# Attention into experts: the last chunk's values ahead of the tenth chunk's gate, three weight splits moved

## The chip, the cores and the metric

The kernel runs on one core of a Trainium2 chip. The time is the device time of one execution in microseconds (us), and the figure of a kernel is the median of its runs. For the kernel before, the three runs shown are 331.6, 331.83 and 452.45 us, so the median is 331.83 us. Its profiled execution is one more run, which took 332.76 us.

## The reference

Three layers follow each other, all in float32.

1. Attention with a decaying state, for 2 x 8 heads, 768 steps and head size 48: `y[t] = r[t] @ (state + (u*k[t]) v[t]^T)`, then `state = w * state + k[t] v[t]^T`.
2. A layer of 8 experts over the 1536 x 384 result: `logits = x @ w_gate`; each token goes to the expert with the largest logit (`argmax`), takes the next free place of that expert in the order of the tokens, and is dropped once the expert's capacity (384) is full; an expert computes `relu(x @ w1[e]) @ w2[e]` with 1024 hidden columns; the result is weighted by the token's softmax probability.
3. A dense layer: `h = x @ w_in`, `h * softmax(h)`, a normalization over the 1024 columns, times `g_ln`, `@ w_out`.

## The kernel before, in words

**Chunks.** Attention works on 12 chunks (`m` = 0 to 11, `NM` = 12) of 128 tokens, six of each batch entry. Below, "chunk 10" is `m` = 10, which the change's title calls the tenth. For each chunk, `values(m)` (L317) and `attend(m)` (carry L330, attended L340) write the output of attention, transposed, into two PSUM tiles; two ScalarE copies `ys` (L346) evict them; `tokens(m)` (L395) turns them back into tokens with the gate's logits beside them (`xp`). `state(m)` (L378, L381) makes the state of the next chunk, and `decay(m)` (L366) scales it ahead.

**The gate.** `gate1(m)` reduces the logits on VectorE (L404 to L414) to a one-hot row of the chosen expert (`oh_all`), then takes the exponentials on ScalarE (`ex`, L417, sum `gs`). `ranks(m)` (L427 to L430) counts, by three small matmuls, the place of each token within its expert. `gate2(m)` takes the reciprocal `gate` (L446), picks the rank (`junk`, L449), makes the slot (L452, L455) and scales the tokens (`whole`, `xg`, L464, ScalarE). `scatter(m)` (L485) writes the slot's table by an indirect DMA on GpSimd, and `store(m)` (L480) the tokens by a DMA on SyncE's queue.

**The first expert's tokens.** The first expert does not wait for its tokens to travel through DRAM. For chunks 0 to 7 they are gathered early (`xe0`, L94, in chunk 9) and transposed into the PSUM tile `x0` (L662). For chunks 8 to 11 they are placed by matmuls: `place(i)` makes a 0/1 matrix `P` (L559, VectorE), `part(i)` and `other(i)` make a high and a low part of the tokens (`xh`, L565 or L568 on ScalarE; `xl`, L574 on GpSimd for chunks 8 to 10, L578 on VectorE for chunk 11), and `add` (L655) adds three matmuls of 224 columns for each chunk and part into `x0`. Then `xhi`, `xlo` (L688, L690) split `x0` for the experts' matmuls.

**Experts.** Each of the 8 experts has four groups `g` of its hidden columns. `mm1(g)` (L813) makes 18 matmuls of 224 columns into `hps`, evicted as `hh` (L819, ScalarE) and `hl` (L820, VectorE). `mm2(g)` (L799 to L801) uses them two groups later. Weights are float32 and come in halves (`raw`, five buffers, L107, SyncE's queue); `split_q(kind, g, ...)` makes of one quarter a high part `whi` (L116, ScalarE) and a low part `wlo` (L122, VectorE). With `defer=True` it issues only the high part and hands back the low part as a function, kept in `pend`. The second expert's tokens are gathered through the slot table (`load_ids`, L86, then `xe`, L94) and transposed by TensorE (`xt`, L792) ahead of `mm2(2)`. A second set of weights (`load_piece`, L140) is decoded on VectorE and ScalarE between the experts' groups.

**Order.** The order of each engine's instructions is that of the program (`manual_schedule`): nothing is rearranged, each engine takes its instructions in turn and waits on semaphores. `together` takes its generators' steps in rotation.

In the kernel before, `split_q(1, 0)` and `split_q(1, 1)` are issued at the end of chunks 4 and 5, their low parts in the middle of chunks 5 and 6; `split_q(2, 0)` is issued in chunk 10 with its low part behind `gate1(10)`. Chunk 11 is the loop's last turn: its `attend` comes behind `gate1(10)`, and `ranks(10)` stands between `attend(11)` and `tokens(11)`.

Of the kernel before, what the change touches and what calls it, by code (L numbers as in the profile page):

```python
# [21 lines left out]
NM = N // C  # L22
# [6 lines left out]
LAST = 4  # L29
# [6 lines left out]
def rwkv_moe_solu_kernel(  # L36
# [75 lines left out]
    def split_q(kind, g, by_dma, defer=False):  # L112
        raw = raw_t[kind, g // 2][:, (g % 2) * 768:(g % 2 + 1) * 768]
        hi = wsp.tile([128, 768], F32R, tag=f"hi{kind}", name=f"whi{kind}_{g}", bufs=2 + kind)
        lo = wsp.tile([128, 768], F32R, tag=f"lo{kind}", name=f"wlo{kind}_{g}", bufs=2 + kind)
        S.activation(hi, raw, AF.Copy)  # L116
        def low():
            if by_dma:
                s = (w1 if kind == 1 else w2)[g // 4, :, g // 2 % 2, (g % 2) * 768:(g % 2 + 1) * 768]
                G.dma_start(out=lo, in_=s, accum_op=ALU.add)  # L120
            else:
                V.tensor_tensor(lo, raw, hi.bitcast(F32), ALU.subtract)  # L122

        if by_dma:
            S.activation(lo, raw, AF.Copy, scale=-1.0)  # L125
        if not defer:
            low()
        n = 3 if kind == 1 else 2
        (w1s if kind == 1 else w2s)[g] = tuple(t.rearrange("p (a f) -> p a f", a=n) for t in (hi, lo))
        return low  # L130
# [5 lines left out]
    def load_piece(p, eng=nc.sync):  # L136
        t = w64_p.tile([128, 384, 2], I32, tag="w64", name=f"w64_{p}")
        s = (w_in if p < NP else w_out).rearrange("p a f -> p (a f)").bitcast(I32)
        j = p % NP
        eng.dma_start(out=t.rearrange("p n c -> p (n c)"), in_=s[:, j * 768:(j + 1) * 768])  # L140
        pieces[p] = t

    def attention(actx):
# [281 lines left out]
        def ranks(m):  # L425
            rp = banks.pop(m)[2]
            T.matmul(rp, mask_b, oh_all[:, m, :], start=True, stop=False)  # L427
            if m:
                T.matmul(rp, ones_b, oh_all[:, m - 1, :], start=False, stop=False)
            T.matmul(rp, ones_b, accs[max(m - 1, 0)], start=False, stop=True)  # L430
            rps[m] = rp
# [3 lines left out]
        def gate2(m):  # L435
            gs = gst.pop(m)
            oh, rk1 = oh_all[:, m, :], rank_all[:, m:m + 1]
            t1 = firsts[m]
            last = m == NM - 1
            if m + 2 < NM:  # L440
                acc = sm.tile([128, NE], BF16, tag="acc", name=f"acc{m}")
                G.tensor_tensor(acc, accs[m], oh, ALU.add)
                accs[m + 1] = acc
            yield
            gate = sm.tile([128, 1], F32, tag="gate", name=f"gate{m}")
            V.reciprocal(gate, gs)  # L446
            raw[m] = xps.pop(m)[:, :, 0:2 * D], gate
            junk = sm.tile([128, NE], F32, tag="junk", name=f"junk{m}")
            V.scalar_tensor_tensor(junk, rps.pop(m), 1.0, oh, ALU.mult, ALU.mult, accum_out=rk1)  # L449
            yield  # L450
            t2 = sm.tile([128, 1], F32, tag="t2", name=f"t2{m}")
            V.tensor_scalar(t2, rk1, float(cap), float(2 * NX), ALU.is_ge, ALU.mult)  # L452
            yield
            slot = sm.tile([128, 1], I32, tag="slot", name=f"slot{m}")
            V.tensor_scalar(slot, rk1, t1, t2, ALU.add, ALU.add)  # L455
            slots[m] = slot
            yield
            if not last:
                whole(m)
            yield  # L460

        def whole(m):
            xg = a2.tile([128, HP, 2 * D], F32, tag="xg", name=f"xg{m}", bufs=LAST + 1)
            S.activation(xg, raw[m][0], AF.Copy, scale=raw[m][1])  # L464
            xgs[m] = xg.rearrange("p a d -> p (a d)")

        def together(*steps):
            steps = list(steps)
            while steps:
                for s in list(steps):  # L470
                    if next(s, steps) is steps:
                        steps.remove(s)
# [82 lines left out]
        onehots, his, los = {}, {}, {}  # L555

        def place(i):
            P0 = sm.tile([128, W], F32R, tag="P0", name=f"P0_{i}", bufs=LAST)
            V.tensor_scalar(P0, iota_w, firsts[i], rank_all[:, i:i + 1], ALU.subtract, ALU.is_equal)  # L559
            return P0  # L560

        def part(i):
            xh = sm.tile([128, DM], F32R, tag="xh", name=f"xh{i}", bufs=LAST)
            if i < NM - 2:
                S.activation(xh, xgs[i], AF.Copy)  # L565
            else:
                xp, gate = raw[i]
                S.activation(xh.rearrange("p (a d) -> p a d", a=HP), xp, AF.Copy, scale=gate)  # L568
            return xh

        def other(i, xh):
            xl = sm.tile([128, DM], F32R, tag="xl", name=f"xl{i}", bufs=LAST)
            if i < NM - 1:
                G.tensor_tensor(xl, xgs[i], xh.bitcast(F32), ALU.subtract)  # L574
            else:
                xp, gate = raw[i]
                three = lambda t: t.rearrange("p (a d) -> p a d", a=HP)
                V.scalar_tensor_tensor(three(xl), xp, gate, three(xh).bitcast(F32), ALU.mult, ALU.subtract)  # L578
            return xl

        halves = {2: (1, 0), 4: (2, 0), 5: (1, 1), 6: (2, 1), 7: (1, 2), 8: (2, 2)}
        first = {4: (1, 0), 5: (1, 1)}
        pend = []
        for m in range(NM):
            values(m)
            if m:
                if m + 1 < NM:
                    scores(m + 1)
                if m + 2 < NM:
                    prelude(m + 2)  # L590
                if m + 1 < NM:
                    mask_scores(m + 1)
            attend(m, lambda: ranks(m - 1) if m else None)
            if m == NM - 2:
                state(m)
            if m == NM - 1:
                onehots[m - 2] = place(m - 2)
                steps = gate2(m - 1)
                for _ in range(4):
                    next(steps)  # L600
                his[m - 1] = part(m - 1)
                together(steps)
            elif m:
                together(gate2(m - 1))
            if m == NM - LAST + 1:
                xe0 = load_xe(0, 0, 2, 1 + (NM - LAST) * C, ld.tile([128, 3, DM], F32, tag="krv", name="xe0"))
            if m:
                scatter(m - 1)
            if m == NM - 1:
                los[m - 1] = other(m - 1, his[m - 1])  # L610
            if m < NM - 2:
                state(m)
            while pend:
                pend.pop()()
            if m == NM - 2:
                pend.append(split_q(2, 0, False, defer=True))
            if m + 2 < NM:
                products = prelude2(m + 2)
                next(products)
            if m < NM - 2:  # L620
                decay(m + 1)
            tokens(m)
            if m + 2 < NM:
                together(gate1(m), products)
                weigh(m + 2)
                prelude3(m + 2)
            elif m + 1 < NM:
                together(gate1(m))
                pend.pop()()
            if NM - LAST < m < NM - 1:  # L630
                if m < NM - 2:
                    onehots[m - 1] = place(m - 1)
                his[m - 1] = part(m - 1)
                los[m - 1] = other(m - 1, his[m - 1])
            chunks.pop(m)
            if m + 4 < NM:
                load_chunk(m + 4)
            if m:
                store(m - 1)
            if m in halves:  # L640
                load_half(*halves[m])
            if m == NM - LAST:
                load_ids(0, 1)
            if m >= NM - 2:
                load_piece(m - NM + 2)
            if m in first:
                pend.append(split_q(*first[m], False, defer=True))


        m = NM - 1  # L650
        x0 = ps_s.tile([128, KD, 256], F32, tag="s", name="x0")[:, :, 0:W]

        def add(i, t):
# [12 lines left out]
        for i in (m - 3, m - 2):  # L666
            add(i, his)
            add(i, los)
        together(gate1(m))
        ranks(m)  # L670
        onehots[m - 1] = place(m - 1)
        steps = gate2(m)
        next(steps), next(steps), next(steps)
        his[m] = part(m)
# [25 lines left out]
    def experts_and_solu():  # L700
# [208 lines left out]
        dec = None  # L909
        most = []  # L910
        split_q(1, 2, False)
        split_q(2, 1, False)
        load_half(1, 3)
        for g in range(NQ + 2):
# [8 lines left out]
            tokens = q == (2 if e else 3) and e + 1 < NE  # L923
# [291 lines left out]
```

## Time and profile before

| | |
|---|---|
| median of the runs shown | 331.83 us |
| the profiled execution | 332.76 us |
| its span, first to last instruction | 331.0 us |
| granted TensorE clock, mean | 0.987 of full |
| TensorE busy | 314.9 us, 95% |
| VectorE busy | 241.8 us, 73% |
| ScalarE busy | 186.5 us, 56% |
| GpSimd busy | 149.7 us, 45% |

The busy shares are means over the whole span. Attention takes its first 77 us, the experts follow until about 216 us, the dense layer is the rest. Times in the rows below are counted from the first instruction. PE is TensorE's matmuls, PEld its weight loads, DVE is VectorE, ACT ScalarE, POOL GpSimd, SP SyncE. A bracket such as `[0.97 <-ACT ex L417]` is the idle time of the engine ahead of the row and what ended it.

### The profile page before, as it was taken

The numbers are of one execution on the slowest core, as the hardware profiler recorded it, in microseconds if no ns is written. First come the engines' busy times: TensorE is split into PE (matmuls) and PEld (weight loads), VectorE is DVE, ScalarE is ACT, GpSimd is POOL, SyncE is SP. The second block draws the span as 40 slices with busy tenths as digits, with TensorE's granted clock in tenths as the row PEclk, the third lists the DMA queues.
The fourth block names the chain that finished last, engine by engine and source line by source line (L and its number), as shares of the span: only waits on it lengthen the run. The fifth ranks groups of instructions, "written<-read, shape, count | busy, mean of one in ns | idle before, by whom it ended". The sixth has DMA issues, their size and how long they took to land. (4 is left out here: it accounts for less than half of the span.)

```text
span 331.0 us, 7339 instructions
## 1 busy us (share of the span) xinstructions
PE 314.9 (95%) x2736; PEld 290.5 (88%) x2736; DVE 241.8 (73%) x555; ACT 186.5 (56%) x406; POOL 149.7 (45%) x198
## 2 busy tenths in 40 slices
PE   8899989969999999999999999999999999999990
PEld 3688778859999999999999999978999999999990
DVE  7899999866999999898999896258745555434310
ACT  2545555556659796868686867126455434444420
POOL 7989899571443232323233364414254222333321
PEclk9999999998999999999999999999999999999996
DMA  6999999342877998988898923100000000000010
GB/s 207 398 331 296 345 386 396 130 142 78 267 282 240 313 297 283 286 290 274 283 282 290 271 70 47 14 2 1 0 26 25 26 24 24 26 24 24 26 48 24
DMA packets 20395, 56.24 MB, mean 170 GB/s; under 512 B 6594, under 2 KB 9028, under 8 KB 20356
## 3 DMA queue, kind: packets, MB, share of 16 engines
q1 hardware_dynamic: 16916, 47.67, 40.9%
q0 software_dynamic: 3440, 8.06, 10.1%
q8 instruction: 23, 0.38, 0.5%
q14 instruction: 16, 0.13, 0.1%
HBM read 50.56 MB, written 5.16 MB: 168 GB/s over the span
## 5 line engine op out<-in xcount | busy, mean ns | idle before, releaser
L122 DVE TENSOR_TENSOR wlo<-raw,whi 128x768 fp32r<-128x768 f32 x57 | 52.4, 954 | 1.5 <-ACT whi L116 1.1
L801 PE MATMUL yps<-hh,wlo 128*128 128x224 f32 x192 | 52.8, 275 | 0.1
L799 PE MATMUL yps<-hh,whi 128*128 128x224 f32 x192 | 52.7, 274 | 0.0
L800 PE MATMUL yps<-hl,whi 128*128 128x224 f32 x192 | 52.6, 274 | 0.0
L116 ACT ACTIVATE whi<-raw 128x768 fp32r<-128x768 f32 x64 | 50.6, 838 | 0.0
L1040 POOL TENSOR_SCALAR e<-e,nmu 128x1024 f32<-128x1024 f32 x12 | 13.5, 1124 | 62.7 <-DVE nmu L1039 59.6
L1017 DVE TENSOR_REDUCE nm<-h 128x1 f32<-128x1024 f32 (+1 forms) x13 | 14.7, 1140 | 33.0 <-PE h L1006 30.0
L801 PEld LDWEIGHTS yps<-hh,wlo 128*128 128x128 f32 x192 | 36.9, 192 | 0.3 <-DMA wlo<-in_w 0.3
L800 PEld LDWEIGHTS yps<-hl,whi 128*128 128x128 f32 x192 | 36.9, 192 | 0.0
L799 PEld LDWEIGHTS yps<-hh,whi 128*128 128x128 f32 x192 | 36.9, 192 | 0.0
L120 POOL DMA_DIRECT2D wlo<-in_w x7 | 6.9, 985 | 64.9 <-ACT wlo L125 64.9
L1074 PE MATMUL o<-w_hi,shi 128*128 128x384 f32 x96 | 33.1, 345 | 0.0
L1075 PE MATMUL o<-w_lo,shi 128*128 128x384 f32 x96 | 32.2, 335 | 0.0
L1076 PE MATMUL o<-w_hi,slo 128*128 128x384 f32 x96 | 32.2, 335 | 0.0
L94 POOL DMA_INDIRECT xe<-xs,ids x16 | 21.0, 1311 | 19.2 <-PE xt L792 8.0
L813 PE MATMUL hps<-xhi,whi 128*128 128x224 f32 x192 | 27.5, 278 | 0.4 <-ACT xhi L688 0.4
L813 PE MATMUL hps<-xlo,whi 128*128 128x224 f32 x192 | 26.7, 275 | 0.0
L813 PE MATMUL hps<-xhi,wlo 128*128 128x224 f32 x192 | 26.6, 274 | 0.0
L819 ACT ACTIVATE hh<-hps 128x448 fp32r<-128x448 f32 x32 | 17.3, 539 | 16.4 <-PE hps L813 15.2
L813 PEld LDWEIGHTS hps<-xhi,whi 128*128 128x128 f32 x192 | 24.1, 192 | 0.6 <-ACT xhi L688 0.5
L813 PEld LDWEIGHTS hps<-xhi,wlo 128*128 128x128 f32 x192 | 24.0, 192 | 0.0
L813 PEld LDWEIGHTS hps<-xlo,whi 128*128 128x128 f32 x192 | 24.0, 192 | 0.0
(183 smaller groups left out, 783.8 us busy)
## 6 DMA issues: line engine op xcount, KB each, us to landing
raw<-in_w SPq DMA_DIRECT2D x32, 768.0 KB
krv<-in_krv SPq DMA_DIRECT2D x11, 576.0 KB
rkT<-in_rkT SPq DMA_DIRECT2D x12, 512.0 KB
w<-in_w_in SPq DMA_DIRECT2D x8, 384.0 KB
w<-in_w_out SPq DMA_DIRECT2D x8, 384.0 KB
wlo<-in_w POOLq DMA_DIRECT2D x7, 384.0 KB
xs<-xg SPq DMA_DIRECT2D x12, 192.0 KB
krv<-in_krv SPq DMA_DIRECT2D x1, 384.0 KB
```

Source lines behind the costliest of these rows:

```text
L94: nc.gpsimd.indirect_dma_start(out=t[0:n, b, :], out_offset=None, in_=xs[0:rows, :], in_offset=bass.IndirectOffsetOnAxis(ap=ids[0:n, e, c: ...
L116: S.activation(hi, raw, AF.Copy)
L122: V.tensor_tensor(lo, raw, hi.bitcast(F32), ALU.subtract)
L799: T.matmul(ps, w[0][ws], x[0][xsl], start=first, stop=False, skip_group_check=True)
L800: T.matmul(ps, w[0][ws], x[1][xsl], start=False, stop=False, skip_group_check=True)
L801: T.matmul(ps, w[1][ws], x[0][xsl], start=False, stop=last, skip_group_check=True)
L813: T.matmul(ps[:, f], w1s[g][i][:, kk, wf], x[j][:, kk], start=not (i or j or f or kk), stop=j == 1 and kk == KD - 1, skip_group_check=True,)
L819: S.activation(hh, ps, AF.Relu)
L1017: V.tensor_reduce(nms[j], ps, AX.X, ALU.max, negate=True)
L1074: T.matmul(ps, hi[:, f % 4], wo[0][:, f], start=f == 0, stop=False)
L1075: T.matmul(ps, hi[:, f % 4], wo[1][:, f], start=False, stop=False)
L1076: T.matmul(ps, lo[:, f % 4], wo[0][:, f], start=False, stop=f == KF - 1)
```

## The change

The loop over chunks ends with `m` = 10. Within chunk 10, `values(11)` and `attend(11)` now stand ahead of `gate1(10)`, without `ranks(10)` in them. Behind the loop come `tokens(11)`, then `ranks(10)`, `place(9)`, the first two steps of `gate2(10)` (the second is the reciprocal, which has a step of its own now) and `part(10)`. Then, as before, the transposes of `xe0`, `add` for chunks 8 and 9, and `gate1(11)`; only behind these the rest of `gate2(10)` with `scatter(10)`, `other(10)`, `store(10)`, `load_piece(1)`, `place(10)` and `ranks(11)`. Since the reciprocal is a step, three steps of `gate2(11)` now reach to the rank; the two small instructions of the slot come behind `other(11)` and `whole(11)`.

Of the weight splits, `split_q(1, 0)` and `split_q(1, 1)` are issued in chunks 5 and 6 behind `state(m)`, with their low parts behind `gate1(m)` of the same chunk; `split_q(2, 0)` is issued at the begin of the experts, between `split_q(1, 2)` and `split_q(2, 1)`.

```diff
             raw[m] = xps.pop(m)[:, :, 0:2 * D], gate
+            yield
             junk = sm.tile([128, NE], F32, tag="junk", name=f"junk{m}")
...
-        first = {4: (1, 0), 5: (1, 1)}
+        first = {5: (1, 0), 6: (1, 1)}
         pend = []
-        for m in range(NM):
+        for m in range(NM - 1):
...
-            if m == NM - 1:
-                onehots[m - 2] = place(m - 2)
-                steps = gate2(m - 1)
-                for _ in range(4):
-                    next(steps)
-                his[m - 1] = part(m - 1)
-                together(steps)
-            elif m:
+            if m:
                 together(gate2(m - 1))
...
-            if m == NM - 1:
-                los[m - 1] = other(m - 1, his[m - 1])
             if m < NM - 2:
                 state(m)
-            while pend:
-                pend.pop()()
-            if m == NM - 2:
-                pend.append(split_q(2, 0, False, defer=True))
+            if m in first:
+                pend.append(split_q(*first[m], False, defer=True))
...
-            elif m + 1 < NM:
+            else:
+                values(m + 1)
+                attend(m + 1, lambda: None)
                 together(gate1(m))
+            while pend:
                 pend.pop()()
-            if NM - LAST < m < NM - 1:
+            if NM - LAST < m:
...
         m = NM - 1
+        tokens(m)
+        ranks(m - 1)
+        onehots[m - 2] = place(m - 2)
+        steps = gate2(m - 1)
+        next(steps), next(steps)
+        his[m - 1] = part(m - 1)
...
         together(gate1(m))
+        together(steps)
+        scatter(m - 1)
+        los[m - 1] = other(m - 1, his[m - 1])
+        store(m - 1)
+        load_piece(1)
+        onehots[m - 1] = place(m - 1)
         ranks(m)
-        onehots[m - 1] = place(m - 1)
...
         split_q(1, 2, False)
+        split_q(2, 0, False)
         split_q(2, 1, False)
```

## Rows read from the trace of the kernel before

**Rows 1.** Windows: busy us of each engine (instructions), PEclk, DMA share, GB/s.
```profile
25.00:50.00 25.00, 23.44 (x363) 19.91 (x362) 23.97 (x77) 13.42 (x50) 23.53 (x24) 1.00 0.97 343
...
69.50:72.90 3.40, 2.02 (x19) 1.92 (x19) 2.38 (x11) 2.55 (x9) 2.62 (x3) 1.00 0.43 124
72.90:76.40 3.50, 3.50 (x21) 3.43 (x20) 2.23 (x10) 1.23 (x5) 1.14 (x2) 0.51 0.60 171
...
78.00:85.00 7.00, 7.00 (x61) 6.87 (x62) 6.21 (x13) 6.20 (x13) 1.36 (x3) 1.00 0.51 143
```

**Rows 2.** Timeline of PE, 68 to 78 us: start, us, engine, line, operation, tiles.
```profile
68.04 1.08 PE L340 MATMUL yp<-A,krv 128*48 128x128 f32 x16
70.09 0.17 PE L427 MATMUL xp<-oh_all,mask_b 128*128 128x8 bf16 x1 [0.97 <-ACT ex L417]
...
71.10 1.14 PE L395 MATMUL xp<-sel,ys 112*128 112x104 f32 x8 [0.79 <-ACT ys L346]
...
73.72 0.84 PE L655 MATMUL x<-P,xh 128*128 128x224 f32 x3
74.36 0.84 PE L655 MATMUL x<-P,xl 128*128 128x224 f32 x3
...
76.47 0.49 PE L655 MATMUL x<-P,xh 128*128 128x224 f32 x3
76.83 0.59 PE L655 MATMUL x<-P,xl 128*128 128x224 f32 x3
...
77.87 1.20 PE L813 MATMUL hps<-xhi,whi 128*128 128x224 f32 x6 [0.37 <-ACT xhi L688]
```

**Rows 3.** Timeline of ACT, chunks 10 and 11.
```profile
69.68 0.27 ACT L417 ACTIVATE ex<-xp,nmx 128x8 f32<-128x8 f32 x1 [0.80 <-DVE oh_all L414]
...
70.69 0.64 ACT L346 ACTIVATE ys<-yp 112x256 f32<-112x256 f32 x2
...
75.54 0.58 ACT L568 ACTIVATE xh<-xp,gate 128x384 fp32r<-128x384 f32 x1 [1.35 <-DVE junk L449]
```

**Rows 4.** Timeline of DVE, chunks 10 and 11.
```profile
67.04 0.36 DVE L381 TENSOR_TENSOR Sc<-st,Sw 128x192 f32<-128x192 f32 x1 [1.82 <-PE xp L395]
...
69.51 0.95 DVE L122 TENSOR_TENSOR wlo<-raw,whi 128x768 fp32r<-128x768 f32 x1
...
71.19 0.27 DVE L455 TENSOR_SCALAR slot<-rank_all,t,t 128x1 int32<-128x1 f32 x1
72.28 0.20 DVE L404 TENSOR_REDUCE xp<-xp 128x8 f32<-128x32 f32 x1 [0.82 <-PE xp L395]
...
73.19 0.23 DVE L414 TENSOR_SCALAR oh_all<-xp,m 128x8 bf16<-128x8 f32 x1
...
75.33 0.17 DVE L449 SCALAR_TENSOR_TENSOR junk<-xp,oh_all 128x8 f32<-128x8 f32 x1 [1.03 <-PE xp L430]
...
76.16 0.62 DVE L578 SCALAR_TENSOR_TENSOR xl<-xp,gate,xh 128x384 fp32r<-128x384 f32 x1
76.69 0.27 DVE L455 TENSOR_SCALAR slot<-rank_all,t,t 128x1 int32<-128x1 f32 x1
```

**Rows 5.** Timeline of POOL, chunks 10 and 11.
```profile
72.03 0.99 POOL L485 DMA_INDIRECT idx<-row,slot  x1 [0.16 <-issue]
73.04 1.02 POOL L574 TENSOR_TENSOR xl<-xg,xh 128x384 fp32r<-128x384 f32 x1
77.23 0.99 POOL L485 DMA_INDIRECT idx<-row,slot  x1 [3.18 <-DVE slot L455]
```

**Rows 6.** Timeline of ACT, chunk 6.
```profile
48.91 0.27 ACT L417 ACTIVATE ex<-xp,nmx 128x8 f32<-128x8 f32 x1 [1.80 <-DVE oh_all L414]
```

**Rows 7.** Timelines of PE and DVE, experts, around the second expert's tokens.
```profile
91.00 0.81 PE L792 MATMUL xt<-ident,xe 128*128 128x128 f32 x6 [0.54 <-DMA xe<-xs,ids]
...
93.68 0.27 PE L799 MATMUL yps<-hh,whi 128*128 128x224 f32 x1
...
91.45 0.62 DVE L820 SCALAR_TENSOR_TENSOR hl<-hps,hh 128x448 fp32r<-128x448 f32 x1
```

More of the change, by code (lines that the diff above doesn't have):

```diff
@@ L643, in attention @@
                 load_ids(0, 1)
[L644 to L647, printed above, removed]
+            if m == NM - 2:
+                load_piece(0)
         m = NM - 1
+        tokens(m)
[4 more added lines that the diff above has]
+        his[m - 1] = part(m - 1)
         x0 = ps_s.tile([128, KD, 256], F32, tag="s", name="x0")[:, :, 0:W]
```

## The prediction

> **What bounds the kernel now.** I read the windows first, because the span's shares mix three layers. In the chunk loop VectorE is busy 23.97 of 25 us and GpSimd 23.53 [rows 1]: the loop goes at VectorE's pace, TensorE and ScalarE have room. In the experts TensorE is busy all 7.0 of 7.0 us [rows 1]: there the end moves only with the time of the first expert matmul, or with a wait that TensorE does not have now. So the change is read where the two meet, from 69 to 78 us, and there the view is the timeline of each engine. TensorE has two holes in it: 0.97 us ahead of `ranks(10)`, which waits for ScalarE's `ex`, and 0.79 us ahead of `tokens(11)`, which waits for the evictions `ys(11)` [rows 2]. The evictions themselves stand behind `ex(10)` on ScalarE [rows 3], though `attended(11)` was done at 68.04 + 1.08 = 69.12 [rows 2]. Behind `tokens(11)` everything follows: `gate1(11)`, `ranks(11)`, rank, `xh`, `xl`, the last `add`, `xhi`, and at 77.87 the first expert matmul [rows 2, 4]. From 72.9 to 76.4 the granted clock is 0.51 [rows 1], the lower of its two levels, and the `add` groups in it are 74.36 - 73.72 = 0.64 us apart against 76.83 - 76.47 = 0.36 behind it [rows 2].
>
> **Part 1, chunk 11's attention ahead of the gate.** On ScalarE, `ys(11)` now follows `whole(9)` and needs `attended(11)` alone, which gives its halves up to 69.12. The pair costs 0.64 [rows 3], of which the first half runs beside the last matmuls: done about 69.5. `tokens(11)` takes 1.14 [rows 2], starts with the first half at about 69.15, and ends near 70.3; now it ends at 72.24. What is pushed back by this: `ex(10)` is queued behind the evictions on ScalarE, but starts at 69.68 as it is, waiting for VectorE [rows 3], so 69.5 costs it nothing (cover 0.15 us; if it is gone, `ex(10)` and the high part of chunk 9 move by as much). `ranks(10)` stands behind `tokens(11)` on TensorE, at about 70.3 for 70.09 [rows 2]; nobody needs it soon now.
>
> `gate1(11)` runs from 72.28 to 73.42 [rows 4], 1.14 us; begun at 70.4 it ends at 71.5. Then the part that comes later than now: `slot(10)` stands behind `gate1(11)` on VectorE. Now it ends at 71.19 + 0.27 = 71.46, that is 1.0 us behind `wlo` (69.51 + 0.95 = 70.46) [rows 4], with `place(9)` and the reciprocal in between; these two are ahead of the gate now, so I estimate 0.75 for the rest, and the slot at about 72.2 (bounds 72.0 and 72.5). Queued behind it on GpSimd are `scatter(10)`, 0.99, and `other(10)`, 1.02 [rows 5]: 72.35 to 73.35 and to about 74.4, for 74.06 now. So the low part of chunk 10 is late by 0.3 us. On SyncE's queue `store(10)` and `load_piece(1)` go out about half a microsecond later, in the same order; the gather that reads those tokens hangs on `scatter(11)`, which is later still, and the piece is decoded in the experts' third group, so this costs nothing.
>
> TensorE: `ranks(10)`, six transposes, four `add` groups at 0.36, so an estimate of 72.4 for `ranks(11)` (the one-hot row is there at 71.5, `ex(11)` by about 72.0), for the wait that ended at 75.33 in `junk(11)` [rows 4]. The rank at 72.7, `xh(11)` 0.58 [rows 3] to 73.5, `xl(11)` 0.62 [rows 4] to 74.1. Slot: two small steps behind it, end about 74.5, for 76.69 + 0.27 = 76.96 [rows 4]; `scatter(11)` at 74.75 for 77.23 [rows 5], 2.5 us earlier. The last three `add` groups wait for the low part of chunk 10 at 74.4, and at 0.36 each plus the tail end at about 75.6. Now they end at 76.83 + 0.59 = 77.42 [rows 2]. So the first expert matmul comes **1.8 us earlier**, at 76.05, if the clock is full.
>
> **Part 2, the split taken out of the tail.** `wlo(2, 0)` is 0.95 us of VectorE [rows 4] between `gate1(10)` and `place(9)`. Its removal is in the times above. At the experts' begin it comes back, as one `whi` on ScalarE and 0.95 us on VectorE ahead of `hl(0)`. Cover: `hl(0)` and the quarter are first used after three groups `mm1` of 18 matmuls, 54 x 0.115 = 6.2 us on (7.0 us for 61 matmuls [rows 1]). The tight place is later, because VectorE stays nearly full (6.21 of 7.0 us [rows 1]): `hl(3)` ends at 91.45 + 0.62 = 92.07, and the matmuls of `mm2(3)` begin at 93.68 [rows 7], 1.6 us of slack. TensorE comes 1.8 us (with the gather below 2.3) earlier, VectorE only 1.8 - 0.95 = 0.85: slack 0.2 to 0.65, just enough. If it is gone the cost is bounded by 0.95. `load_half(1, 3)` on SyncE's queue waits for one split more, which the same 0.85 leaves earlier than now.
>
> TensorE's one wait in the experts' beginning is 0.54 us for the gather of the second expert's tokens [rows 7], which hangs on `scatter(11)`. That is 2.5 us earlier while TensorE is 1.8 earlier, 0.7 to the good: between 0 and 0.54 saved, and I take **0.5**.
>
> **Part 3, the two splits in chunks 5 and 6.** Same instructions, same VectorE time, placed behind the gate instead of ahead of it; VectorE sets the pace and has no hole there. The `whi` leaves the place ahead of the evictions and comes ahead of `decay`, where ScalarE sits idle 1.80 us before `ex` [rows 6]. Zero, bounds -0.3 to +0.3, since GpSimd is as full as VectorE and the two may collide in another place.
>
> Kept as it is: VectorE's 1.82 us ahead of the state of chunk 11 [rows 4], whose cause no row shows; it lies ahead of all that part 1 moves. Bounds for it: nothing, or 1.8 gained if it depends on the neighbourhood.
>
> **The sum.** Against the profiled execution: 332.76 - 1.8 - 0.5 = 330.4 us. The median of the runs, 331.83, lies 0.93 under that execution. The half-clock stretch would explain just that: three groups that decide the rank's time lose 0.28 each, 0.85. If the other runs lack it, then 1.8 shrinks to 0.9 and 331.83 - 0.9 - 0.5 = 330.4 again. If the profile simply adds 0.93, it is 331.83 - 2.3 = 329.5. I take **330.4 us**.
>
> **Rivals.** *A: the half clock moves into the experts* (ends slower than before). In my times TensorE has a hole from 73.0 to 74.4, where it waits for GpSimd's low part of chunk 10. In the trace the clock fell at 72.9, behind a stretch in which TensorE was busy for 2.02 of 3.4 us [rows 1]. If such a hole sends it down again, 3.5 us at half clock fall on expert matmuls that have no slack: 21 matmuls went in 3.5 us there against 61 in 7.0 at full [rows 1], so 9.5 matmuls of 0.115 are lost, 1.1 us, or by the clock alone half of 3.5, 1.75. With 1.7: 330.4 + 1.7 = 332.1. What decides is how long `other(10)` keeps TensorE waiting: with the low part at 73.3 there is no hole, and no rival. Against it: the hole stands alone, between full stretches, and the holes now are two, 1.76 us together [rows 2]. [...]
>
> *B: the gain stays in the tail* (the change does not do what it says). `add` for chunk 10's low part hangs on `gate1(11)`, `slot(10)`, `scatter(10)`, `other(10)` in a row, a chain of 1.14 + 0.75 + 0.99 + 1.02 that I start at 70.4. If `tokens(11)` is held up, say by the evictions coming behind `ex(10)` after all, the chain ends near 76 and `x0` no earlier than now: 331.8, with the gather's half a microsecond 331.3. For it: the chain is made longer. Against: the evictions need nothing but `attended(11)`.
>
> *C: VectorE's lag reaches TensorE* at `hl(3)`: up to 0.95 of the gain lost, 331.3.
>
> **How the numbers follow.** Forecast (329.3 to 331.0) 0.55; A (331.4 to 332.2) 0.22; B 0.12; C 0.06; 0.05 for what I do not see, half of it above 332.2. The range runs from 329.2, the sum without the profile's extra and with part 3's bound, to 332.1, rival A, and leaves out less than 2 in 10. A change under 2%, 6.6 us, is no change for a measurement of this kernel, and all cases but the unseen lie within it: faster 0.02, same 0.96, slower 0.02.
>
> **What will show it.** Right: `ys(11)` before `ex(10)` on ScalarE; `tokens(11)` ending near 70.3; `gate1(11)` ahead of `slot(10)` on VectorE; the last `add` about 1.8 us earlier, waiting for POOL's `xl`; no wait of TensorE for `xe`. A would show as a PEclk near 0.5 after 74 us; B as a last `add` near 77; C as TensorE waiting for `hl` around 90 us. What would make me wrong outright is a stall that appears or goes in code that the change does not touch, such as the 1.82 us.

## The result, and the profile after

The changed kernel takes 335.71 us (median of 4 runs, 334.87 to 336.6), the kernel before 331.72 us (4 runs): ratio 1.0125, 95% interval 1.0091 to 1.0159. One of the four runs before took 452.45 us and is left out of the ratio. The changed kernel is 4 us slower, where 1.4 us faster had been forecast. The profiled executions took 335.65 and 332.76 us, their spans are 333.9 and 331.0 us. These 2.9 us can be split at three points that both traces have:

| stretch | before | after | difference |
|---|---|---|---|
| first instruction to the reciprocal of chunk 8 | 60.00 | 64.02 | +4.02 |
| from there to the first expert matmul | 17.87 | 15.83 | -2.04 |
| from there to the second expert's transposes `xt` | 13.13 | 14.07 | +0.94 |
| from there to the end | 240.0 | 240.0 | 0 |

The 4.0 us of the timed runs are as much as the first stretch alone. The 2.04 us that the profile wins back behind it are about as much as one stall: VectorE's 1.82 us ahead of the state of chunk 11 [rows 4], which this one execution of the changed kernel does not show. No run separates the two.

Line numbers of the profile after are one higher than before from L449 to about L600, three lower in the tail's matmuls, and two higher in the experts.

**Where the 4 us are.** The timelines of VectorE, GpSimd and TensorE of the changed kernel in chunk 5 (start, duration, engine, line, operation; the bracket is idle time ahead of it and what ended it), and one row of chunk 6:

```profile
42.36 0.54 DVE L285 TENSOR_TENSOR vab<-krv,ra 128x384 f32<-128x384 f32 x1
42.82 3.17 DVE L122 TENSOR_TENSOR wlo<-raw,whi 128x768 fp32r<-128x768 f32 x1
45.92 1.21 DVE L304 TENSOR_TENSOR A<-sp,mask 128x1024 f32<-128x1024 f32 x1
...
50.48 2.82 DVE L122 TENSOR_TENSOR wlo<-raw,whi 128x768 fp32r<-128x768 f32 x1
...
42.85 1.18 POOL L262 TENSOR_TENSOR rt<-rkT,TB 128x512 f32<-128x512 f32 x1
43.99 1.18 POOL L262 TENSOR_TENSOR kt<-rkT,TB 128x512 f32<-128x512 f32 x1
45.13 0.91 POOL L442 TENSOR_TENSOR acc<-acc,oh_all 128x8 bf16<-128x8 bf16 x1
...
44.67 0.60 PE L317 MATMUL yp<-ident,vab 128*112 128x128 f32 x4
47.27 0.94 PE L297 MATMUL sp<-rt,kt 64*128 64x128 f32 x12 [2.01 <-DVE junk L450]
```

The low part `wlo` takes 3.17 and 2.82 us in place of 0.95 [rows 4]. It ends 0.82 us after GpSimd's second product `kt` has ended at 45.17: it stood still while `rt` and `kt` ran back to back, and then did its work. Behind it VectorE is late with the masked scores `A`, and TensorE waits 2.01 us (and 1.66 in chunk 6). VectorE standing still is shown here as busy: from 25 to 50 us its busy time is 23.97 of 25 in both traces, but with 74 instructions where there were 77 [rows 1].

```profile
25.00:50.00 25.00, 22.74 (x344) 19.36 (x344) 23.97 (x74) 12.66 (x44) 21.63 (x23) 1.00 0.98 346
...
80.70:84.10 3.40, 3.40 (x19) 3.40 (x18) 3.33 (x9) 1.97 (x4) 0.13 (x1) 0.51 0.09 14
84.20:91.20 7.00, 7.00 (x64) 7.00 (x64) 6.25 (x13) 5.80 (x10) 3.86 (x6) 1.00 0.90 273
```

These are windows of the changed kernel, columns as in [rows 1]. The lower two show the forecast's rival A: the granted clock is 0.51 from 80.7 to 84.1 (before it was 0.50 from 73.0 to 76.3 in windows of 0.1 us, and 1.00 on both sides), now in expert matmuls, and TensorE gets 19 of them done in 3.4 us, against 64 in 7.0 us at 1.00 behind it.

**The tail**, in the timelines of TensorE, ScalarE, VectorE and GpSimd of the changed kernel, beside [rows 2 to 5]:

```profile
72.08 1.14 PE L395 MATMUL xp<-sel,ys 112*128 112x104 f32 x8
...
74.79 0.69 PE L659 MATMUL x<-ident,xe 96*128 96x96 f32 x5 [1.35 <-DMA xe<-xs,ids]
...
78.14 0.59 PE L652 MATMUL x<-P,xl 128*128 128x224 f32 x3 [0.79 <-POOL xl L575]
...
79.85 1.34 PE L815 MATMUL hps<-xhi,whi 128*128 128x224 f32 x6 [0.37 <-ACT xhi L690]
...
71.64 0.82 ACT L346 ACTIVATE ys<-yp 112x256 f32<-112x256 f32 x2 [1.39 <-PE yp L340]
72.36 0.26 ACT L417 ACTIVATE ex<-xp,nmx 128x8 f32<-128x8 f32 x1
...
69.15 0.34 DVE L381 TENSOR_TENSOR Sc<-st,Sw 128x192 f32<-128x192 f32 x1
...
73.25 0.20 DVE L404 TENSOR_REDUCE xp<-xp 128x8 f32<-128x32 f32 x1
...
74.69 0.28 DVE L456 TENSOR_SCALAR slot<-rank_all,t,t 128x1 int32<-128x1 f32 x1
74.88 1.16 DVE L560 TENSOR_SCALAR P<-iota_w,t,rank_all 128x224 fp32r<-128x224 f32 x1
...
74.86 1.04 POOL L575 TENSOR_TENSOR xl<-xg,xh 128x384 fp32r<-128x384 f32 x1
76.06 0.99 POOL L486 DMA_INDIRECT idx<-row,slot  x1 [0.17 <-DVE P L560]
77.07 1.02 POOL L575 TENSOR_TENSOR xl<-xg,xh 128x384 fp32r<-128x384 f32 x1
```

The order is the one the forecast described: `ys(11)` ahead of `ex(10)`, `tokens(11)` directly behind the attended values, `gate1(11)` ahead of `slot(10)`. VectorE's 1.82 us ahead of the state [rows 4] are gone here. New are 1.35 us in which TensorE waits for the gather of `xe0`, and 0.79 us for GpSimd's low part of chunk 10.

### The profile page after: what moved, and what is told of

It is laid out like the page before. It is cut to its first block, busy times and chain, and to the rows that moved or that the text cites. A ratio compares the mean times of both kernels' runs of the same rounds, so it can differ in the third digit from the quotient of the medians.

```text
span 333.9 us, 7339 instructions
## 1 busy us (share of the span) xinstructions
PE 315.4 (94%) x2736; PEld 290.9 (87%) x2736; DVE 246.6 (74%) x555; ACT 187.1 (56%) x406; POOL 149.8 (45%) x198
## 5 line engine op out<-in xcount | busy, mean ns | idle before, releaser
L122 DVE TENSOR_TENSOR wlo<-raw,whi 128x768 fp32r<-128x768 f32 x57 | 56.3, 1021 | 1.6 <-ACT whi L116 1.1
L815 PEld LDWEIGHTS hps<-xhi,wlo 128*128 128x128 f32 x192 | 24.7, 196 | 0.0
L815 PEld LDWEIGHTS hps<-xlo,whi 128*128 128x128 f32 x192 | 24.7, 196 | 0.0
```

Of the source, the lines that this page charges most:

```text
L815: T.matmul(ps[:, f], w1s[g][i][:, kk, wf], x[j][:, kk], start=not (i or j or f or kk), stop=j == 1 and kk == KD - 1, skip_group_check=True,)
```

## The experiments

Theory 1: the two low parts, put beside GpSimd's `rt` and `kt`, cost the 4 us, and the reordered tail gives little. Rival: the high part's new place on ScalarE, or the tail, costs it. "Splits back" below is the changed kernel with both quarters split in their old places. Ratios are to the kernel before, on the same chip, and are taken over the runs and not from the medians, so the two can differ a little.

| kernel | median us | ratio, 95% interval |
|---|---|---|
| 1 splits back | 332.75 | 1.0011 (0.9990 to 1.0033) |
| 2 before, and only the two splits moved | 336.65 | 1.0122 (1.0063 to 1.0181) |
| 3 changed, low parts alone moved back | 332.59 | 1.0006 (0.9990 to 1.0022) |
| 4 changed, `wlo` reads scores from PSUM | 339.78 | 1.0218 (1.0186 to 1.0249) |
| 5 changed, `wlo` reads products from PSUM | 332.65 | 1.0004 (0.9982 to 1.0026) |
| 6 splits back, `xl(10)` on VectorE | 332.64 | 1.0014 (0.9989 to 1.0038) |
| 7 splits back, gathers of `xe0` later | 334.33 | 1.0044 (1.0024 to 1.0065) |
| 8 both of 6 and 7 | 333.97 | 1.0066 (1.0036 to 1.0095) |
| 9 before, `xe0` by a plain transfer | 330.84 | 0.9959 (0.9938 to 0.9981) |
| 10 splits back, `xe0` by a plain transfer | 332.39 | 0.9998 (0.9969 to 1.0027) |
| 11 splits back, `xl(10)` ahead of its scatter | 331.57 | 0.9982 (0.9958 to 1.0005) |
| 12 the one before, with spare matmuls | 331.76 | 0.9984 (0.9963 to 1.0004) |
| 13 11 with late gathers, `x0` reordered | 330.19 | 0.9945 (0.9920 to 0.9971) |
| 14 before, with 13's late gathers and `x0` order | 332.52 | 0.9987 (0.9961 to 1.0014) |
| 15 13 again, beside 14 | 332.11 | 1.0007 (0.9982 to 1.0033) |

**1, 2 and 3: which part costs.**

```diff
-        first = {5: (1, 0), 6: (1, 1)}
+        first = {4: (1, 0), 5: (1, 1)}
...
+            while pend:             # 1 and 3: low part back behind state(m)
+                pend.pop()()
...
-            while pend:             # from behind the gate
-                pend.pop()()
...
+            if m in first:          # 1 only: high part back at the chunk's end
+                pend.append(split_q(*first[m], False, defer=True))
```

Number 3 keeps `first` and the high part's new place; number 2 puts both new places into the kernel before.

> The changed kernel with the two quarters of chunks 4 to 6 put back where they were (high part at the end of chunks 4 and 5, low part behind the next chunk's state); tail and experts' begin as changed. Theory 1 (the low part, with both operands in SBUF, stands still on VectorE while GpSimd makes rt and kt beside it, 2.2 + 1.85 us): 4.0 us faster than the changed kernel, near 331.7, and both wlo near 0.99 us again. Theory 2 (the loss is in the tail and the experts: GpSimd's chain, the half clock): stays within 1 us of 335.7.

> The kernel before with nothing but the two quarters moved behind the gates of chunks 5 and 6. Theory 1: 4.0 us slower than before, near 335.7, wlo of 2.8 to 3.2 us in chunks 5 and 6. Theory 2: same as before, 331.7. If both the loop and the tail matter, e1 and e2 add up: their distances from the kernel before sum to 4.0.

> The changed kernel with only the low parts (VectorE) put back behind the next chunk's state; the high parts (ScalarE) stay in the new place. Theory 1 says that the low part's place alone costs: near 331.7. Rival within the loop (the moved high part on ScalarE delays ex and the evictions): stays near 335.7.

With the splits back the 4 us are gone; put alone into the kernel before, they are there; and the low part alone is enough. The reciprocal of chunk 8 comes at 60.39, 64.18 and 60.43 us (60.00 and 64.02 in the two traces above). In number 3 one of the two low parts still meets the end of `kt`, and stands for the 0.5 us of it that are left (VectorE and GpSimd, timelines):

```profile
44.78 1.32 DVE L122 TENSOR_TENSOR wlo<-raw,whi 128x768 fp32r<-128x768 f32 x1
...
44.12 1.17 POOL L262 TENSOR_TENSOR kt<-rkT,TB 128x512 f32<-128x512 f32 x1
45.26 0.90 POOL L442 TENSOR_TENSOR acc<-acc,oh_all 128x8 bf16<-128x8 bf16 x1
```

**4 and 5: what in the low part stands still.** The place stays, the first operand changes (the low weights of two quarters of the first expert are wrong by it).

```diff
-                V.tensor_tensor(lo, raw, hi.bitcast(F32), ALU.subtract)
+                V.tensor_tensor(lo, scores, hi.bitcast(F32), ALU.subtract)            # 4
+                V.tensor_tensor(lo, ra_columns_twice, hi.bitcast(F32), ALU.subtract)  # 5
```

> The changed kernel, but the low parts of these two quarters subtract from a score tile in PSUM in place of the raw weights in SBUF (so two quarters of the first expert's low weights are other numbers): same place, same length, same engine, one SBUF operand in place of two. Theory 1: no standstill beside GpSimd's rt and kt, wlo near 1.0 us, 331.7. Rival (the place behind the gate costs by itself, whatever the operands): wlo stays at 2.8 to 3.2 us and the time at 335.7.

> The changed kernel, with one thing different: in chunks 5 and 6 the subtraction that gives a quarter's low part (wlo) takes as its first operand, in place of the quarter in SBUF, the 384 columns of the product tile ra in PSUM, read twice. Same place in the order, same size of output; the low weights of two quarters of the first expert are wrong by this. VectorE wrote ra itself, so no wait for another engine is added. Theory 1 (wlo stands still because it reads both operands from SBUF while GpSimd's rt and kt run): wlo takes 0.95 to 1.0 us in both places, in place of 3.17 and 2.82, acc takes 0.19 in place of 0.91, and the time is that of the kernel before, 332.6 (bounds 332.0 to 333.3). Rival (the place is dear in itself, whatever wlo reads, say by the order of the steps behind it): wlo short or long, the time stays near 336.

In number 4 the standstill went (0.95 us), but the time is a miss, 8 us above the 331.7 expected: the stand-in held the score tile, so that TensorE's scores waited for `wlo`, and VectorE's mask behind them 2.26 and 1.35 us, a wait of the experiment's own making. Number 5 reads a tile that VectorE wrote itself. Its timelines of VectorE and GpSimd in chunk 5 (line numbers up to seven higher):

```profile
43.15 0.95 DVE L124 TENSOR_TENSOR wlo<-ra,whi 128x768 fp32r<-128x768 f32 x1
44.01 1.21 DVE L311 TENSOR_TENSOR A<-sp,mask 128x1024 f32<-128x1024 f32 x1
...
43.18 1.18 POOL L268 TENSOR_TENSOR rt<-rkT,TB 128x512 f32<-128x512 f32 x1
44.33 1.18 POOL L268 TENSOR_TENSOR kt<-rkT,TB 128x512 f32<-128x512 f32 x1
45.47 0.19 POOL L449 TENSOR_TENSOR acc<-acc,oh_all 128x8 bf16<-128x8 bf16 x1
```

Same place, same size, `rt` and `kt` beside it as before, and `wlo` takes 0.95 us, `acc` 0.19 instead of 0.91; the time is that of the kernel before. So in this place it is the reading of two operands from SBUF that stands still beside GpSimd's products: `wlo` took 3.17 us with both operands in SBUF and 0.95 with one in PSUM, and it waited out two GpSimd instructions in a row, `rt` and `kt` of 1.18 us each. By what means the two hold each other up, and what decides which of them waits, no run shows.

**6 to 8: GpSimd's queue in the tail.** With the splits back the first expert matmul is at 76.95; TensorE waits 1.20 us for `xl(10)`.

```diff
-            if i < NM - 1:      # other(): low part on GpSimd
+            if i < NM - 2:      # 6, 8
...
-            if m == NM - LAST + 1:      # 7, 8: from ahead of scatter(8) ...
-                xe0 = load_xe(...)
...
+            if m == NM - LAST + 1:      # ... to behind other(8)
+                xe0 = load_xe(...)
```

> The changed kernel with both quarters split in their old places, and besides chunk 10's low part xl(10) made on VectorE, not on GpSimd. In the kernel with the quarters alone put back TensorE waits 1.19 us for GpSimd's xl(10) (74.17 to 75.18), and VectorE's place(11) takes 1.36 us beside it. Theory (GpSimd's chain of slot, scatter and low part of chunk 10 holds the last add groups): the first expert matmul comes about 0.7 us earlier than 76.95, and the time falls by as much, from 332.75 to 332.0. Rival (what the tail gains is taken by the half clock or by the experts' first waits): the first expert matmul is earlier and the time stays at 332.6 to 332.8.

> The changed kernel with both quarters split in their old places, and besides the gathers of the first expert tokens (xe0) issued on GpSimd's queue in chunk 9 behind the low part's work of chunk 8, not ahead of the scatter. Theory (GpSimd's queue stands at the gather's wait for its ids, and the work behind it is late; TensorE's 1.01 us ahead of tokens(11) comes of it): scatter(8) starts earlier, the hole ahead of tokens(11) shrinks, the time falls by up to 0.5, to 332.2. Rival (GpSimd has room there): no change, 332.75. Slower if the gather comes to land behind the transposes of x0: up to 0.5, 333.2.

Number 6 is a miss: TensorE's wait for GpSimd became one of 1.12 us for VectorE, whose `place(10)` now stands behind `xl(10)`; first expert matmul at 76.85. Number 7 is slower, by 0.8 to 2.2 us: TensorE waits 1.77 and 0.68 us for the gather ahead of `x0`. But `tokens(11)` ends at 69.50 for 71.13: the hole ahead of it has gone. Number 8 adds both, for which 331.5 to 332.0 had been expected, and is as slow.

**9 and 10: the gather taken away.** `xe0` comes by one transfer of another input, so the first expert works on wrong tokens in that part.

```diff
-                xe0 = load_xe(0, 0, 2, 1 + (NM - LAST) * C, ld.tile(...))
+                xe0 = ld.tile([128, 3, DM], F32, tag="krv", name="xe0")
+                nc.sync.dma_start(out=xe0[:, 0:2], in_=krv[:, 0, 0:2])
```

> The kernel before, with one thing different: the first expert's tokens (xe0) are not gathered on GpSimd's queue in chunk 9, but as many bytes of another input are loaded by one plain transfer on SyncE's queue (the first expert works on wrong tokens in the part that xe0 brings). Theory (the gather under way is what holds TensorE's results back around 65 to 69 us): VectorE's 1.82 us ahead of Sc(11) are gone, under 0.4, and the first expert matmul comes up to 1.5 us earlier than 77.87, the time at 331.1 to 332.0. Rival (the stall is the chain of that stretch, or any transfer): Sc(11) still waits 1.0 to 1.9 and the time is 332.6.

> The same in the changed kernel with both quarters split in their old places: xe0 by a plain transfer of another input in place of the gather. Theory: gate1(10) does not wait 1.06 and tokens(11) not 1.01 us; tokens(11) ends near 69.5, as where the gathers were put behind, the first expert matmul comes at 75.5 to 76.2 in place of 76.95, and the time is 331.3 to 332.0. Rival: the same holes, first expert matmul at 76.5 to 77.0, time 332.6.

In the kernel before it did what theory said: VectorE's stall is gone (first row below, timelines of number 9; 1.82 in [rows 4]), the first expert matmul is 2.7 us earlier, the time 0.6 to 2.1 us lower. GpSimd's scatter and low part of chunk 8 come 1.7 to 1.8 us earlier too (65.12 and 66.15, for 66.84 and 67.91), so this is not the stall's worth alone.

```profile
65.08 0.36 DVE L381 TENSOR_TENSOR Sc<-st,Sw 128x192 f32<-128x192 f32 x1
...
75.16 1.69 PE L814 MATMUL hps<-xhi,whi 128*128 128x224 f32 x6 [0.37 <-ACT xhi L689]
```

In the new order it failed (first expert matmul at 77.58, for 75.5 to 76.2 expected): 0.7 us of the hold-up stayed (the second `ys(11)` waits for TensorE until 69.73), `ex(10)` behind it held VectorE 2.16 us, and the profile has 6.8 us at the lower clock from 75.1 (mean clock 0.982; the last two `add` groups start at 75.65 and 76.29, 0.64 us apart, where two of the earlier ones, at 72.09 and 72.43, are 0.34 apart). The gather is not the whole cause.

**11 and 12: the low part first, and spare matmuls.**

```diff
-        scatter(m - 1)
         los[m - 1] = other(m - 1, his[m - 1])
+        scatter(m - 1)
...
+        fill(6)                       # 12: transposes into an unread tile
         tokens(m)
...
+            fill(4 if i < m else 0)   # 12: between chunk 10's high and low part
```

> The changed kernel with both quarters split in their old places, and in the tail chunk 10's low part xl(10) ahead of its scatter on GpSimd. Theory (GpSimd's chain slot, scatter, low part holds the last groups): xl(10) ends at 74.55 in place of 75.18, VectorE's place(11) and xl(11) behind it follow, the first expert matmul comes 0.5 to 0.65 us earlier than 76.95, and the time falls from 332.7 to 332.1. Rival: the gain is lost at the experts' begin (wait for the second expert's gather, which scatter(11) does not bring earlier), time 332.6.

> The one before, and six spare transposes of 0.11 us on TensorE ahead of tokens(11) and four ahead of the last low part of chunk 10, into a tile that nobody reads. Theory (the holes of TensorE in the tail send the clock to its lower level in some executions, and that costs 0.6 us on the average): no stretch of half clock between 60 and 100 us, mean clocks of the runs at 0.992 or above, and the time 0.4 to 0.7 lower than the one before, 331.5. Rival (the half clock has another cause or costs nothing): the time as the one before, or 0.1 to 0.3 higher by the spare work.

Number 11 does as expected in its profile (`xl(10)` ends at 73.97, first expert matmul 75.74), and its median is 0.8 us lower, with an interval that still holds no change. Part of its gain is lost where its rival said, at the second expert's gather: `scatter(11)` comes at 75.43, only 0.31 us ahead of the first expert matmul (0.64 in the kernel before), and TensorE waits twice at `xt` (timeline of number 11; 0.54 in [rows 7]):

```profile
89.37 0.52 PE L794 MATMUL xt<-ident,xe 128*128 128x128 f32 x3 [1.03 <-DMA xe<-xs,ids]
90.29 0.44 PE L794 MATMUL xt<-ident,xe 96*128 96x96 f32 x3 [0.41 <-DMA xe<-xs,ids]
```

Number 11 shows the stall at the state again, though nothing ahead of it differs from number 1, which shows it in two other places (timelines, 11 then 1):

```profile
67.28 0.36 DVE L381 TENSOR_TENSOR Sc<-st,Sw 128x192 f32<-128x192 f32 x1 [1.83 <-PE xp L395]
```

```profile
65.79 0.36 DVE L381 TENSOR_TENSOR Sc<-st,Sw 128x192 f32<-128x192 f32 x1 [0.19 <-PE st L378]
...
67.91 0.20 DVE L404 TENSOR_REDUCE xp<-xp 128x8 f32<-128x32 f32 x1 [1.06 <-PE xp L395]
...
69.99 1.14 PE L395 MATMUL xp<-sel,ys 112*128 112x104 f32 x8 [1.01 <-ACT ys L346]
```

With the spare matmuls the mean granted clock is 0.991 or more in each of the 12 runs. But number 11 had that in 10 of its 12 without them, so that they keep the clock up is not shown, and the time does not fall.

**13 to 15: the gather late, with other work for TensorE.**

```diff
+            if m == NM - LAST + 1:      # behind other(8), as in 7
+                xe0 = load_xe(...)
+            if m == NM - 2:             # scatter(9) behind other(9)
+                scatter(m - 1)
...
+        first_tokens()                  # xe0 @ identity, start=False, behind ranks(11)
         for i in (m - 1, m):
```

The expectations below call this place the low part of chunk 9; the edit issues the gathers behind that of chunk 8.

> The one with chunk 10's low part ahead of its scatter, and besides: the gathers of xe0 issued behind the low part of chunk 9 on GpSimd's queue, the scatter of chunk 9 behind them, and on TensorE the part of x0 that xe0 brings added behind the groups of chunks 8 and 9 and behind ranks(11), by plain matmuls with the identity. Theory (TensorE's results are held back while the gather is under way with work behind them; with it late nothing is held back, and TensorE has other work until it lands): no wait over 0.5 us of VectorE at Sc(11) or at gate1(10), the first expert matmul at 74.6 to 75.2 for 75.74, the time 0.5 to 1.0 us below the one before (331.6), that is 330.6 to 331.1. Rival (the hold-up comes with the order of the tail, not with the gather): the same 1.0 to 1.9 us in another place, first expert matmul at 75.7 or later, time 331.6 or more.

> The kernel before (old order: chunk 11 in the loop, chunk 10's gate ahead of chunk 11's attention, the split of the second matrix's quarter in the tail), with the late gather as in the fast version: gathers of xe0 behind the low part of chunk 9, the scatters of chunks 9 and 10 behind their low parts, xe0's part of x0 behind the groups of chunks 8 and 9 and behind ranks(11). Theory (the hold-up beside the gather is what the end of the loop loses, and the order of the tail is worth under 0.5 us): the same time as the fast version, 330.2 (bounds 329.8 to 330.8), no wait at Sc(11). Rival (the new order is worth its 1 to 1.8 us once the hold-up is gone): 331.2 to 332.0.

> The fast version once more, beside the one with the old order, for a profile of an ordinary execution: time 330.2, ratio 0.993 to 0.996; no wait over 0.5 us at Sc(11) and at gate1(10), first expert matmul at 74.6 to 75.2.

Number 13 was the fastest, 1.0 to 2.7 us under the kernel before by its interval; run again on another chip as number 15, the same program was level with it, at 332.11 for the 330.2 expected. So no version with the right tokens is shown to be faster. In the profile of number 15 nothing waits at the state or at `gate1(10)`, but VectorE waits 1.12 us for TensorE at `gate1(11)`; the first expert matmul is at 75.99. Number 14 missed its 330.2 too (332.52): VectorE waits only 0.37 us at its state, but `ys(11)` starts 1.8 us after `attended(11)` has ended. Between the orders, 14 and 15 on one chip, 0.4 us lie in the medians, the ratios lie the other way round, and their intervals overlap: which order is better is not shown.

## Why the prediction was wrong, step by step

- **Part 3, the two splits in chunks 5 and 6: this step failed.** It was put at zero, -0.3 to +0.3, "since GpSimd is as full as VectorE and the two may collide in another place". The collision was named and not priced: it is 2.18 + 1.83 us in the two rows of `wlo` above, against 0.99 each before, and +4.02 at the reciprocal of chunk 8. The same instructions did not take the same time. Rows of the kernel before that the forecast does not use show the collision both ways (VectorE and GpSimd, timelines):

```profile
40.06 0.99 DVE L122 TENSOR_TENSOR wlo<-raw,whi 128x768 fp32r<-128x768 f32 x1
...
63.69 0.39 DVE L559 TENSOR_SCALAR P<-iota_w,t,rank_all 128x224 fp32r<-128x224 f32 x1
...
73.33 0.87 DVE L559 TENSOR_SCALAR P<-iota_w,t,rank_all 128x224 fp32r<-128x224 f32 x1
...
40.19 0.91 POOL L442 TENSOR_TENSOR acc<-acc,oh_all 128x8 bf16<-128x8 bf16 x1
...
68.89 0.19 POOL L442 TENSOR_TENSOR acc<-acc,oh_all 128x8 bf16<-128x8 bf16 x1
```

  A sum of 8 columns that takes 0.91 us beside `wlo` and 0.19 elsewhere; a `P` that takes 0.87 beside GpSimd's low part [rows 5] and 0.39 elsewhere. There `wlo` had been placed beside the cheapest GpSimd work of the chunk; the change put it beside the dearest, 2.3 us of products. With such rows read as waits the price could have been estimated from above: if the wait lasts as long as the GpSimd work beside it, 2.3 us each time.
- **Part 3, the high part** cost nothing, as said (number 3).
- **Part 1, the order,** came as described, and from `gate1(11)` on also in its size: with the splits back, `xl(10)` ends 4.0 us after `gate1(11)` begins, and 4.0 had been worked out. But in the timed runs parts 1 and 2 together give nothing: with the splits back -0.3 to +1.1 us, where -1.4 against the median had been forecast. What the runs show in its place: `tokens(11)` ends at 71.13, not 70.3, because TensorE's results come late once more, now at `gate1(10)` and `ys(11)` in place of the state; 0.39 of the 0.8 us is there already at the reciprocal of chunk 8 (60.39 for 60.00). I had kept the 1.82 us "as it is", ahead of all that moves; it is not bound to that place. In the profile of number 1 the first expert matmul is still 0.92 us earlier than before, at 76.95, but the span only 0.2 shorter. 0.4 of it is a wait of TensorE that the profile before does not have, for ScalarE's `yThi`, the eviction of the last expert; for the rest the cause is not shown.
- **The cover of `ex(10)`** (0.15 us) was gone: without the stall `oh(10)` is ready at 71.23 and `ex(10)` starts at 72.36 behind the evictions; the reciprocal waits 1.44 us for it. It cost nothing, since `gate1(11)` could not start earlier anyway.
- **Part 2** held for `hl`: TensorE does not wait for it (rival C). The 0.5 us of the second expert's gather did not come. In the changed kernel TensorE has no wait for `xe` at `xt`, but there the lower clock (0.51 from 80.7 to 84.1) brings TensorE to it late. In number 1, without such a stretch (mean clock 0.992) and with `scatter(11)` as far ahead of the first expert matmul (0.45 us in both), it waits 0.61 us, more than before. `scatter(11)` was to be 2.5 us earlier, TensorE 1.8; they are 0.73 (76.50 for 77.23) and 0.92. The rank of chunk 11 is later than worked out (`junk` ends at 73.82, for 72.7), and behind it `place(11)`, ahead of `xl(11)` and the slot, takes 1.36 us beside GpSimd's `xl(10)`, against 0.40 in the kernel before: one more collision that the sum had at nothing (number 1, timelines of VectorE, GpSimd and TensorE):

```profile
73.96 1.36 DVE L560 TENSOR_SCALAR P<-iota_w,t,rank_all 128x224 fp32r<-128x224 f32 x1
...
74.17 1.01 POOL L575 TENSOR_TENSOR xl<-xg,xh 128x384 fp32r<-128x384 f32 x1
76.50 0.99 POOL L486 DMA_INDIRECT idx<-row,slot  x1 [1.32 <-DVE slot L456]
...
90.14 1.00 PE L794 MATMUL xt<-ident,xe 128*128 128x128 f32 x6 [0.61 <-DMA xe<-xs,ids]
```

- **Rival A** came on top, in the profile at least: a clock of 0.51 in the first expert groups. 0.94 us more to `xt`, and the 0.54 of the gather's wait that are not there [rows 7], make 1.5 us lost; 1.7 had been estimated, with a chance of 0.22. Number 1 keeps the new tail and has no such stretch in its profile (mean clock 0.992), so it does not follow from the order alone. Nor is it shown that a hole sends the clock down: from 73.0 to 76.4 TensorE was busy 2.05 of 3.4 us in the changed kernel, and the clock read 1.00 until 80.7.
- **Rival B** came in part, by another way than it named: with the splits back `tokens(11)` is held up, but by `ys(11)` waiting for TensorE until 69.56 and not by `ex(10)`, and the last `add` ends at 76.50, between the 75.6 of the sum and the 77.42 of before. TensorE's wait for `xl(10)` is no sign of it; the sum had that wait too.

That the change stays under 2% came true by the size of the loss alone, and not by the forecast's reasons; the time lies 3.6 us above the range.

## What to carry to other kernels

Before an instruction is moved on a full engine, list what runs beside it in the new place on VectorE and GpSimd, and where its operands lie; an instruction of VectorE with two operands in SBUF was paid here with the whole GpSimd work beside it (`wlo`, 3.17 us for 0.95). Look in the trace for one line with two durations: here it showed the collision as busy time, with no wait ahead of `wlo` in the list of waits. And the stall that no row explains was not fixed to its place here (`Sc(11)` at 67.04 in the kernel before, `gate1(10)` at 67.91 in number 1); a gain behind it should be counted only down to zero.

## What the runs showed of the hardware that was not expected

- VectorE's `wlo` did not get in between two GpSimd instructions in the changed kernel: 2.18 and 1.83 us of standstill, through `rt` and `kt`.
- VectorE's `place`, 0.39 to 0.40 us elsewhere, took 0.87, 1.07 and 1.36 us beside GpSimd's low part (kernel before, numbers 11 and 1). What in it stands still was not tested.
- In all but a few of the traces one or two results of TensorE reach their reader 0.5 to 2.5 us after the end of their matmuls, which the profile models, around 65 to 75 us, at places that change between executions (before: `Sc(11)`; number 1: `gate1(10)` and `ys(11)`; number 15: `gate1(11)`). It was absent in number 9, without the gather, and in the changed kernel, with it; a smaller one, 0.70 us at `ys(11)`, was in number 10, without it. In nine traces (before and numbers 1, 3, 4, 5, 7, 11, 14, 15) one late reader starts 1.40 to 1.52 us after the second gather of `xe0` starts on GpSimd, wherever the gather stands (before: 65.55 and 67.04; number 15: 69.16 and 70.66); numbers 2, 6, 8, 12 and 13 do not show it. The cause stays open.
- The granted clock: of 127 runs of the kernel before, the 42 with a mean of 0.988 or less have a median of 332.85 us, the 32 with 0.993 or more 331.6. The 1.25 us between them are about as much as the reordering was to bring; the runs come from several chips, and that the lower clock is the cause is not shown.
